# Stores of the inverse's rows moved from SP's queue to ScalarE's, and the last two pairs of out tiles loaded by SP inside the loop

## The chip, the cores and the metric

The kernel runs on one core of one Trainium2 chip. Its time is the device time of one execution in microseconds (us); the time before is the median of three executions, 530.65 us (528.84 to 531.64). The profile shown is that of one more execution.

## What is computed

Two branches work on 2048 rows of 512 channels and are mixed by a gate that each row computes for itself. Branch `a` is a long convolution (a state space model): each channel has a filter of 2048 taps, and the product with the signal is made in the frequency domain. Branch `b` is a two-layer network with a gelu between.

```python
x = A_u                                             # 1 x 2048 x 512
g = sigmoid((x * gate_w).sum(-1, keepdims=True))
# a: taps K[d, l] = Re sum_n C[d,n] * exp(dt*A[d,n]*l) * dt*B[d,n];  y = irfft(rfft(u) * rfft(K)) + u * Dskip
a = _A_ref(x, A_re, A_im, B_re, B_im, C_re, C_im, log_dt, Dskip)
h = gelu(einsum("bsd,df->bsf", B_x, w1) + b1)       # F = 1792
b = einsum("bsf,fd->bsd", h, w2) + b2
return g * a + (1 - g) * b
```

## The kernel before

The kernel has two parts. `front` (0 to about 418 us of the profiled span) makes the network, the filter's taps and the first stage of both transforms; a planner sets its order, and nothing in it changes here. It leaves `(1 - g) * b` in the output tensor for most rows, the half-transformed signal in the DRAM tensor `tu_d`, the half-transformed taps in `tk_d`, and a few products of the network (`late`) still to do.

`conv` is written out by hand, in program order, with no planner. Its tiles are 128 x 512 floats (256 KB). It has sixteen steps `s`, each for two of 32 slices, then a tail. In step `s`:

- SP loads what later steps need: tap slices (`fetch`, L1110), constants `cc` (L1102), signal slices (L1241).
- `product(s)`, on VectorE: six operations on the signal `pu` (PSUM) and the taps `k`.
- `signal(s + 1)`, on TensorE (L1129): eight matmul rows of the trace into two PSUM tiles, named `p2u`.
- `matrices(s // 2 + 1)`, in even steps up to 12: ScalarE makes from a `cc` tile the two halves of a matrix `f1` (L1117, L1118, shown as `f`).
- `taps(s + 2)`: TensorE makes `p2k` for `c` = 0 (with a part of `cc`) and `c` = 1 (with `f1`), and ScalarE copies each to `k` (L1137).
- `inverse(s)`: TensorE makes two PSUM tiles `pa` (L1168).
- `turn(s)`: ScalarE copies each `pa` into one of six buffers `sa` (L1174), and SP stores it in the DRAM tensor `t4_d` (L1176; `t_d<-sa` in the profile). After each eighth slice the rows of that group are read back in another layout into `den` and `t3` (L1188): by GpSimd for the first three groups, by ScalarE for the last.
- In steps 7 to 12 SP loads one pair of output tiles back (`dense`, L1202: 512 KB, from the output tensor into a place in `attic` or `loft` whose signal slices are used up). These are the six pairs of `HERE`.

After the loop ScalarE issues the loads of the two pairs in `THERE` (pair 4 into `loft`, pair 5 into `attic`), and TensorE does 18 of the left-over products of the network (L1213 to L1215; three more are done in step 15). Then for each of eight pairs `m` TensorE makes two tiles `pb` (L1273) out of `den` or `t3`, VectorE (L1285) or ScalarE with GpSimd (L1282, L1283) add them to the pair's tiles, and the pair is stored in the output: by SP (L1289), the last pair half by SP and half by ScalarE (L1287).

PSUM has one buffer for each of `p2k` 0 and 1 and `pa` 0 and 1; `k` and `f1` have two buffers each.

An engine runs its instructions in program order, and a DMA that it issues is one of them. What an instruction has to wait for are semaphores. The program deals the DMAs that SP and ScalarE issue round eight of these, called DMAHW0 to DMAHW7, in the order in which the program was laid out; a DMA waits until the one before it on its semaphore, eight DMAs earlier, has landed, unless its engine has already waited for that one.

Of the kernel before, what the change touches and what calls it, by code (L numbers as in the profile page):

```python
# [73 lines left out]
HERE, THERE = (7, 6, 0, 1, 2, 3), (4, 5)  # L74
# [201 lines left out]
def gated_mix(  # L276
# [18 lines left out]
    nc = tc.nc  # L295
# [5 lines left out]
    t4_d = dr.tile([4, 2, GROUP, 2, 32, D], F32, name="t4_d")  # L301
# [789 lines left out]
    def conv(pool, ps, late, attic, loft, den):  # L1091


        sas = [pool.tile([P, D], F32, name=f"sa{k}", bufs=1) for k in range(6)]
# [75 lines left out]
        def turn(s):  # L1170

            for n in (2 * s, 2 * s + 1):
                sa = sas[n % 6]
                nc.scalar.copy(sa, pas.pop(n))  # L1174
                g, k = divmod(n, GROUP)
                nc.sync.dma_start(t4_d[g, :, k].rearrange("e c q d -> (c q) e d"), sa)  # L1176
                if k < GROUP - 1:
                    continue
                rows = t4_d[g].rearrange("e k c q d -> (e k c) q d")

                for h in (0, 4, 8, 16, 24) if g == 3 else (0, 8, 16, 24):
                    if h == 24 and g < 2:
                        held.append((t3[g:P:4, 16:24], rows[:, 24:32]))
                        continue
                    on = nc.gpsimd if n < 31 else nc.scalar
                    e = h + (4 if g == 3 and h < 8 else 8)
                    to = t3[g:P:4, h - 8 : e - 8] if h > 7 else den[g:P:4, h:e]
                    on.dma_start(to, rows[:, h:e])  # L1188
# [4 lines left out]
        def dense(k, on):  # L1193

            q = HERE.index(k) if k in HERE else 6 + THERE.index(k)
            r = 5 + 2 * q if q < 7 else 0
            if r < N_ATTIC:
                mos[k] = attic[:, r : r + 2]
            else:
                r -= N_ATTIC  # L1200
                mos[k] = loft[:, r * D : (r + 2) * D].rearrange("p (s d) -> p s d", s=2)
            on.dma_start(mos[k], out[2 * k : 2 * k + 2].rearrange("s p d -> p s d"))  # L1202

        def rest(n):

            while late and n:
                s, h, l, w, wl = late.pop(0)
                first = s not in accs
                last = not any(e[0] == s for e in late)
                if first:  # L1210
                    accs[s] = ps.tile([P, D], F32, tag=f"pu{s}" if s > 1 else f"pk{s}", name=f"acc{s}", bufs=1)
                ss = slice(s % 2 * P, s % 2 * P + P)
                nc.tensor.matmul(accs[s], h[:, ss], w, start=first, stop=False)  # L1213
                nc.tensor.matmul(accs[s], h[:, ss], wl, start=False, stop=False)
                nc.tensor.matmul(accs[s], l[:, ss], w, start=False, stop=last)  # L1215
                n -= 1
# [13 lines left out]
        for s in range(16):  # L1230

            for n in range(2 * s + N_TK + (2 if s else 0), 2 * s + N_TK + 4):
                if n < 24:
                    fetch(n if n < 16 else n + 8)
            if s == 0:
                for n in range(16, 24):
                    fetch(n)
            if s in (2, 4, 6, 8):
                consts(s // 2 + 3)
            for n in range(2 * s + N_ROOM, min(2 * s + N_ROOM + 2, 32)) if s > 3 else ():  # L1240
                nc.sync.dma_start(us[n], tu_d[ko[n]])  # L1241
            product(s)
            if s + 1 < 16:
                signal(s + 1)
            if s + 2 < 16:
                if s % 2 == 0:
                    matrices(s // 2 + 1)
                taps(s + 2)
            if s == 9:
                for to, rows in held:  # L1250
                    nc.gpsimd.dma_start(to, rows)
            if s == 15:
                rest(N_REST)
            inverse(s)
            turn(s)
            if 7 <= s < 13:
                dense(HERE[s - 7], nc.sync)
        for k in THERE:
            dense(k, nc.scalar)
        rest(18)  # L1260

        for s in range(4):
            m, i = 7 - s // 2, s % 2
            z, g = mos[m][:, i], gate[:, 1, 2 * m + i : 2 * m + i + 1]
            nc.vector.scalar_tensor_tensor(z, accs[s], g, z, ALU.mult, ALU.add)

        for m in range(8):
# [9 lines left out]
            for i in range(2):  # L1277
                t = 2 * m + i
                z, g = mos[m][:, i], gate[:, 0, t : t + 1]
# [21 lines left out]
    with (  # L1301
        tc.tile_pool(name="fp", bufs=2, reuse_waits="tile") as fp,
        tc.tile_pool(name="ps_f", bufs=2, space=PSUM, reuse_waits="tile") as ps_f,
    ):
        conv(fp, ps_f, late, attic, loft, den)
# [64 lines left out]
```

## Time and profile before

| | us |
|---|---|
| median of three executions | 530.65 (528.84 to 531.64) |
| the profiled execution | 528.3 |
| its span | 526.5 |
| TensorE (PE) busy in the span | 509.1 (97%) |
| VectorE (DVE) busy | 428.4 (81%) |
| ScalarE (ACT) busy | 353.0 (67%) |
| GpSimd (POOL) busy | 41.6 (8%) |
| `conv`: first `p2k` matmul to last `pb` matmul | 418.3 to 520.0 |

The columns of a timeline row are the start and the length in us from the span's start, the engine, the line, the operation and its tiles, how many are merged in the row, and in brackets how long the engine was idle just before and what ended that. PE is the matmul side of TensorE, PEld its weight loads; SPq and ACTq are instructions of the SP and ScalarE queues that only issue DMAs or wait, and they are not counted as busy. Buffer numbers are left out of names, so `t` is `t3` or its like, and `t_d` is `t4_d`. Rows of DMAs give how many, the size of one and the median time from issue to landing.

### The profile page before, as it was taken

The numbers are of one execution on the slowest core, as the hardware profiler recorded it, in microseconds if no ns is written. First come the engines' busy times: TensorE is split into PE (matmuls) and PEld (weight loads), VectorE is DVE, ScalarE is ACT, GpSimd is POOL, SyncE is SP. The second block draws the span as 40 slices with busy tenths as digits, with TensorE's granted clock in tenths as the row PEclk, the third lists the DMA queues.
The fourth block names the chain that finished last, engine by engine and source line by source line (L and its number), as shares of the span: only waits on it lengthen the run. The fifth ranks groups of instructions, "written<-read, shape, count | busy, mean of one in ns | idle before, by whom it ended". The sixth has DMA issues, their size and how long they took to land.

```text
span 526.5 us, 12296 instructions
## 1 busy us (share of the span) xinstructions
PE 509.1 (97%) x4858; PEld 387.8 (74%) x4858; DVE 428.4 (81%) x808; ACT 353.0 (67%) x614; POOL 41.6 (8%) x80
## 2 busy tenths in 40 slices
PE   8887999999999999999999999999999999999995
PEld 7656789898889978976988998988988722222551
DVE  6898899999999968879999989999901188777543
ACT  4989946699875689986595998456534545565311
POOL 2000000000000000000012001202010100110123
PEclk9999999999999999999999999999999999999998
DMA  8999664152685434392879026625669899999978
GB/s 241 369 301 285 222 223 153 67 202 54 159 224 201 142 91 132 111 300 86 220 156 301 3 81 126 159 40 121 201 202 172 226 309 319 366 347 375 301 277 329
DMA packets 82517, 107.87 MB, mean 205 GB/s; under 512 B 39334, under 2 KB 43562, under 8 KB 81916
## 3 DMA queue, kind: packets, MB, share of 16 engines
q1 hardware_dynamic: 76476, 85.04, 50.8%
q0 software_dynamic: 5056, 18.65, 14.0%
q10 hardware_dynamic: 928, 3.41, 1.8%
q8 instruction: 38, 0.62, 0.5%
q14 instruction: 19, 0.16, 0.1%
HBM read 61.46 MB, written 45.62 MB: 203 GB/s over the span
## 4 chain that ended last, share of the span: by engine, by line
PE 75%; ACT 11%; DMA 8%; DVE 3%; issue 2%; SPq 1%; ACTq 0%; DVEq 0%
PE pk L693 10%; PE ph L915 8%; PE ph L917 8%; PE ph L916 8%; PE acc L965 8%; PE acc L967 7%; PE acc L966 7%; PE p2u L1129 6%; PE p2k L1129 5%; PE pa L1168 3%; PE pb L1273 3%; DMA tu_d<-attic 2%; PE ph L415 2%; ACT L932 2%; ACT ph L932 2%
## 5 line engine op out<-in xcount | busy, mean ns | idle before, releaser
L915 PE MATMUL ph<-xh,wh 128*128 128x256 f32 x448 | 128.1, 286 | 2.9 <-ACT attic L433 1.8
L917 PE MATMUL ph<-xh,wl 128*128 128x256 f32 x448 | 127.0, 284 | 0.5 <-DVE wl L794 0.4
L916 PE MATMUL ph<-xlo,wh 128*128 128x256 f32 x448 | 126.6, 283 | 0.0
L915 PEld LDWEIGHTS ph<-xh,wh 128*128 128x128 f32 x448 | 85.1, 190 | 11.9 <-issue 5.6
L916 PEld LDWEIGHTS ph<-xlo,wh 128*128 128x128 f32 x448 | 85.2, 190 | 2.0
L917 PEld LDWEIGHTS ph<-xh,wl 128*128 128x128 f32 x448 | 85.1, 190 | 1.2 <-DVE wl L794 1.2
L965 PE MATMUL acc<-wh,hh 128*128 128x512 f32 x206 | 82.9, 403 | 1.3 <-ACT hh L935 1.2
L967 PE MATMUL acc<-wh,hl 128*128 128x512 f32 x206 | 81.1, 394 | 0.4 <-DVE hl L945 0.4
L966 PE MATMUL acc<-wl,hh 128*128 128x512 f32 x206 | 80.9, 393 | 0.0
L932 ACT ACTIVATE ph<-ph,b1t 128x256 f32<-128x256 f32 x112 | 50.4, 450 | 43.3 <-PE ph L917 41.3
L945 DVE TENSOR_TENSOR hl<-ph,hh 128x512 fp32r<-128x512 f32 (+1 forms) x62 | 38.3, 618 | 31.9 <-ACT hh L935 31.6
L693 PE MATMUL pk<-y,den 128*32 128x64 f32 x2048 | 61.4, 290 | 0.0
L693 PEld LDWEIGHTS pk<-y,den 128*32 128x32 f32 x2048 | 57.2, 136 | 3.7 <-issue 1.4
L965 PEld LDWEIGHTS acc<-wh,hh 128*128 128x128 f32 x206 | 38.7, 188 | 15.9 <-issue 6.8
L967 PEld LDWEIGHTS acc<-wh,hl 128*128 128x128 f32 x206 | 38.7, 188 | 10.6 <-DVE hl L945 2.0
L655 DVE TENSOR_TENSOR y<-y,ea 128x64 f32<-128x64 f32 (+4 forms) x80 | 45.2, 566 | 0.2
L966 PEld LDWEIGHTS acc<-wl,hh 128*128 128x128 f32 x206 | 38.7, 188 | 6.5
L935 ACT CAST hh<-ph 128x512 fp32r<-128x512 f32 (+1 forms) x62 | 33.0, 533 | 8.7 <-PE acc L966 5.2
L500 DVE TENSOR_TENSOR loft<-den,zz 128x256 f32<-128x256 f32 (+2 forms) x48 | 37.2, 775 | 1.7 <-ACT den L626 1.3
L501 DVE TENSOR_TENSOR loft<-den,zz 128x256 f32<-128x256 f32 (+2 forms) x48 | 37.1, 773 | 0.0
L668 DVE TENSOR_TENSOR y<-y,loft 128x2048 f32<-128x2048 f32 x16 | 36.5, 2283 | 0.0
L1137 ACT COPY k<-p2k 128x512 f32<-128x512 f32 x32 | 18.8, 586 | 24.9 <-issue 13.1
(183 smaller groups left out, 885.2 us busy)
## 6 DMA issues: line engine op xcount, KB each, us to landing
tu_d<-attic SPq DMA_DIRECT2D x64, 128.0 KB, 3.6
tk_d<-sk SPq DMA_DIRECT2D x32, 256.0 KB, 4.7
t_d<-sa SPq DMA_DIRECT2D x32, 256.0 KB, 6.8
tk<-tk_d SPq DMA_DIRECT2D x24, 256.0 KB, 4.9
t<-t_d POOLq DMA_DIRECT2D x9, 512.0 KB, 8.3
attic<-in_xt_dram SPq DMA_DIRECT2D x16, 256.0 KB, 4.4
xh_d<-xh SPq DMA_DIRECT2D x8, 512.0 KB, 3.2
xl_d<-xlo SPq DMA_DIRECT2D x8, 512.0 KB, 4.9
```

What stands on the lines that cost most here:

```text
L500: vec(2 * m, lambda: vv.tensor_mul(t, a, br), due, [ka, *kb], [kt])
L655: nc.vector.tensor_mul(both(n, 64 - 3 * n, n), both(0, 64 - n, n), an)
L693: nc.tensor.matmul(pks[q][32 * j : 32 * j + 32, :, gg], x[:, r, :, ch], y[:, r, :, ch], start=(r == 0), stop=(r == 1), skip_group_check=True,)
L915: nc.tensor.matmul(p, h, xh[xk][:, d], start=(d == 0), stop=False)
L916: nc.tensor.matmul(p, h, xlo[xk][:, d], start=False, stop=False)
L917: nc.tensor.matmul(p, lo, xh[xk][:, d], start=False, stop=(d == 3))
L932: nc.scalar.activation(phs[q][:, n], phs[q][:, n], AF.Gelu_apprx_tanh, bias=b1t[:, f : f + 1])
L945: nc.vector.tensor_sub(lo, phs[q][:, 0:nf], hi.bitcast(F32))
L965: nc.tensor.matmul(a, h, wh[1][w], start=start, stop=False)
L966: nc.tensor.matmul(a, h, wl[1][w], start=False, stop=False)
L967: nc.tensor.matmul(a, l, wh[1][w], start=False, stop=(j == 3))
L1129: nc.tensor.matmul(out[64 * i : 64 * i + 64], w, x, start=True, stop=True)
```

## The change

`turn` first makes both copies, and then ScalarE itself issues both stores. SP issues none of them any more. The two loads of `THERE` go from ScalarE, after the loop, to SP, at the ends of steps 14 and 15.

```diff
@@ turn(s)
             for n in (2 * s, 2 * s + 1):
                 sa = sas[n % 6]
                 nc.scalar.copy(sa, pas.pop(n))
+            for n in (2 * s, 2 * s + 1):
                 g, k = divmod(n, GROUP)
-                nc.sync.dma_start(t4_d[g, :, k].rearrange("e c q d -> (c q) e d"), sa)
+                nc.scalar.dma_start(t4_d[g, :, k].rearrange("e c q d -> (c q) e d"), sas[n % 6])
                 if k < GROUP - 1:
                     continue
                 rows = t4_d[g].rearrange("e k c q d -> (e k c) q d")
@@ the loop over s
             turn(s)
             if 7 <= s < 13:
                 dense(HERE[s - 7], nc.sync)
-        for k in THERE:
-            dense(k, nc.scalar)
+            if s > 13:
+                dense(THERE[s - 14], nc.sync)
         rest(18)
```

Three places in the built program show what moves. The first is ScalarE at the end of step 1 and the start of step 2, where the copies to `sa` are followed by the two halves of `f`. Before:

```order
L1174 COPY sa_4794<-pa_4937 128x512 [waits PE_49]
L1174 COPY sa_4795<-pa_4940 128x512 [waits PE_49]
L1117 ACTIVATE f_4967<-cc_4814 64x256 [waits DMAHW0_49]
L1118 COPY f_4967<-cc_4814 64x256
L1137 COPY k_4973<-p2k_4970 128x512 [waits DVE_49,PE_49,Activation_49]
```

After:

```order
L1174 COPY sa_4794<-pa_4937 128x512 [waits PE_49]
L1174 COPY sa_4795<-pa_4940 128x512 [waits PE_49]
L1177 DMA t_d<-sa_4794 64x2x512 [waits DMAHW2_49,Activation_49]
L1177 DMA t_d<-sa_4795 64x2x512 [waits DMAHW3_49,Activation_49]
L1117 ACTIVATE f_4967<-cc_4814 64x256 [waits DMAHW0_49]
L1118 COPY f_4967<-cc_4814 64x256
L1137 COPY k_4973<-p2k_4970 128x512 [waits DVE_49,PE_49]
```

Both stores now stand between the copies and `f`; each waits for its copy and for one of the eight semaphores. In the changed program the DMA that last used DMAHW2 is the seventh of the eight `t3` loads of step 0, which SP issues, and that of DMAHW3 is the second store of step 0. At the end of step 5, the next place of this kind that matters below, the two stores wait for a tap load of SP's in step 5 and for the first store of step 4.

The second place is SP in steps 0 to 2, from the last two `t3` loads on (`tk` are tap slices). Before:

```order
L1110 DMA t_4806<-tk_d 128x512 [waits DMAHW1_49]
L1110 DMA t_4806<-tk_d 128x512 [waits DMAHW2_49]
L1176 DMA t_d<-sa_4792 64x2x512 [waits DMAHW3_49,Activation_49]
L1176 DMA t_d<-sa_4793 64x2x512 [waits DMAHW4_49,Activation_49]
L1110 DMA tk_4909<-tk_d 128x512 [waits DMAHW5_49,PE_49]
L1110 DMA tk_4911<-tk_d 128x512 [waits DMAHW6_49,PE_49]
L1176 DMA t_d<-sa_4794 64x2x512 [waits DMAHW7_49,Activation_49]
L1176 DMA t_d<-sa_4795 64x2x512 [waits DMAHW0_49,Activation_49]
```

After:

```order
L1110 DMA t_4806<-tk_d 128x512 [waits DMAHW2_49]
L1110 DMA t_4806<-tk_d 128x512 [waits DMAHW4_49]
L1110 DMA tk_4909<-tk_d 128x512 [waits DMAHW5_49,PE_49]
L1110 DMA tk_4911<-tk_d 128x512 [waits DMAHW6_49,PE_49]
L1110 DMA tk_4947<-tk_d 128x512 [waits DMAHW7_49,PE_49]
L1110 DMA tk_4949<-tk_d 128x512 [waits DMAHW0_49,PE_49]
```

SP's loads no longer stand behind a wait for ScalarE's copies; they wait only for a semaphore of the eight and for TensorE to be through with the buffer.

The third place is ScalarE behind the last copies of step 15. Before:

```order
L1174 COPY sa_4793<-pa_5469 128x512 [waits DMAHW6_49,PE_49,Activation_49]
L1188 DMA den<-t_d 32x2048 [waits DMAHW3_49,DMAHW4_49,DMAHW2_49,DMAHW5_49,DMAHW1_49,DMAHW0_49]
L1188 DMA den<-t_d 32x2048 [waits DMAHW7_49]
L1188 DMA t_4806<-t_d 32x4096 [waits DMASW6_49,DMASW5_49]
L1188 DMA t_4806<-t_d 32x4096 x2
L1202 DMA loft<-out_dram 128x2x512
L1202 DMA attic<-out_dram 128x2x512
L1282 ACTIVATE sa_4792<-pb_5536,gate 128x512 [waits PE_49,Activation_49]
```

After:

```order
L1174 COPY sa_4793<-pa_5470 128x512 [waits DMAHW0_49,PE_49]
L1177 DMA t_d<-sa_4792 64x2x512 [waits DMAHW6_49,Activation_49]
L1177 DMA t_d<-sa_4793 64x2x512 [waits Activation_49]
L1189 DMA den<-t_d 32x2048 [waits DMAHW5_49,DMAHW6_49,DMAHW4_49,DMAHW7_49,DMAHW3_49,DMAHW2_49]
L1189 DMA den<-t_d 32x2048 [waits DMAHW1_49]
L1189 DMA t_4806<-t_d 32x4096 [waits DMASW6_49,DMASW5_49]
L1189 DMA t_4806<-t_d 32x4096 x2
L1283 ACTIVATE sa_4792<-pb_5536,gate 128x512 [waits PE_49]
```

The two `THERE` loads are gone from behind the reads of the last group; on SP they are now the last two DMAs ahead of the output's stores, with nothing between them and the six `HERE` loads.

## Prediction

> **What bounds the kernel now.** I read the busy times by stretch of the convolution first, then the chain of work that ended last, then the timeline of TensorE and ScalarE over one loop step, then the DMA landings.
>
> ```profile
> 440.00:460.00 20.00, 20.00 (x106) 5.50 (x102) 16.33 (x28) 11.05 (x21) 1.59 (x3) 1.00 0.94 330
> 460.00:480.00 20.00, 20.00 (x108) 5.47 (x108) 16.31 (x27) 11.53 (x23) 2.57 (x5) 1.00 0.98 354
> ...
> 496.51 6.42 DMA t_d<-sa
> ...
> 503.02 2.87 DMA den<-t_d
> ...
> 506.02 13.97 PE pb L1273 x64
> ```
>
> The first two rows are stretches of the loop (length, then busy time of PE, PEld, DVE, ACT, POOL; granted clock; DMA share; GB/s). TensorE is busy for all 20.00 us, so whatever delays it in the loop is lost. ScalarE has 11 of 20 us of work. The DMA engines are 94 to 98% busy. The other rows are the chain: behind the loop it runs over the last copy's store, the read back, then the 64 `pb` matmuls.
>
> **ScalarE's extra work.** The change gives ScalarE two DMA issues per step. At the end of even steps the next thing that ScalarE does is a `k` copy, 1.7 us later. At the end of odd steps `f` comes next, and TensorE needs it soon. One place of each kind, with SP's stores of the first:
>
> ```profile
> 479.83 1.07 ACT L1174 COPY sa<-pa 128x512 f32<-128x512 f32 x2 [0.39 <-PE pa L1168]
> 480.93 0.41 ACT L1117 ACTIVATE f<-cc 64x256 f32<-64x256 f32 x1
> 481.36 0.40 ACT L1118 COPY f<-cc 64x256 f32<-64x256 f32 x1
> 482.62 0.59 ACT L1137 COPY k<-p2k 128x512 f32<-128x512 f32 x1 [0.86 <-ACT f L1118]
> ...
> 481.47 1.03 PE L1129 MATMUL p2k<-tk,cc 128*64 128x512 f32 x4
> 482.33 1.03 PE L1129 MATMUL p2k<-tk,f 128*64 128x512 f32 x4
> 483.29 1.09 PE L1168 MATMUL pa<-v,cc 64*64 64x512 f32 x8
> ...
> 480.45 1.21 SPq L1176 DMA_DIRECT2D t_d<-sa  x2
> 484.44 1.07 ACT L1174 COPY sa<-pa 128x512 f32<-128x512 f32 x2 [0.39 <-PE pa L1168]
> 487.19 0.59 ACT L1137 COPY k<-p2k 128x512 f32<-128x512 f32 x1 [1.68 <-issue]
> ```
>
> `f` is done at 481.76 and TensorE multiplies with it at 482.33: 0.57 us to spare. What a late `f` does, the first `taps` shows, and what an issue costs on ScalarE, the tail shows:
>
> ```profile
> 419.72 0.40 ACT L1118 COPY f<-cc 64x256 f32<-64x256 f32 x1
> 420.17 1.08 PE L1129 MATMUL p2k<-tk,f 128*64 128x512 f32 x4 [0.80 <-ACT f L1118]
> 421.08 1.03 PE L1129 MATMUL p2u<-den,cc 128*64 128x512 f32 x4
> ...
> L1188 ACTq DMA_DIRECT2D t<-t_d x3: 550/615/616, 504.3 to 505.5; - x3
> L1188 ACTq DMA_DIRECT2D den<-t_d x2: 521/559/597, 503.0 to 503.6; - x2
> ...
> L1202 ACTq DMA_DIRECT2D loft<-out_dram x1: 785/785/785, 506.2 to 506.2; - x1
> L1202 ACTq DMA_DIRECT2D attic<-out_dram x1: 652/652/652, 507.0 to 507.0; - x1
> ...
> L1137 ACTq EVENT_SEMAPHORE  x2: 17/1324/2631, 484.5 to 488.0; - x2
> ```
>
> TensorE starts 0.05 us after `f` ends (420.12 to 420.17), and the next block starts 0.91 us later (421.08), where undelayed blocks follow each other by 0.86 (481.47 to 482.33). ScalarE's seven issues of these rows (shortest, median, longest in ns) add up to 4.34 us, 0.62 each; SP's two stores take 1.21 with their gaps, about 0.55 each. ScalarE's own rows are nearer: 1.30 for two, with gaps. The last row says that ScalarE's queue was waiting at 484.5 for the next `k` copy while the two `sa` copies (from 484.44 on) still ran, so its sequencer runs ahead of its engine; the first store can be issued beside the second copy, at 480.45 as on SP. Then both are out at 481.75; `f` starts some 0.06 later and needs 0.83: 482.64. TensorE goes on at 482.69 in place of 482.33, and loses 0.05 more: 0.41. Over six places (ends of steps 1, 3, 5, 7, 9, 11) that is **+2.5 us**. From below: issues of 0.38 (the shortest of ScalarE's, quoted further down) leave `f` in time, 0. From above: if the first issue starts only when both copies are through, at 480.93, each place costs 0.48 more, 5.3 in all. I take the middle value because the waiting row bears on that very question.
>
> At the end of even steps the second issue ends at 484.44 + 0.62 + 1.30 = 486.4 and the `k` copy starts at 487.19: the idle 1.68 us hide it. If that cover went, `k` would come late to `product`, which uses it only in the next step but one.
>
> **The new waits.** Behind a store that waits for its semaphore stand `f`, the `k` copies and the next `sa` copies; TensorE waits for `f` within 0.6 us, for the others within more than 1. So waits count after steps 1 and 5, where what is waited for is young:
>
> ```profile
> 425.67 3.82 SPq L1110 DMA_DIRECT2D t<-tk_d  x8
> 433.80 1.07 ACT L1174 COPY sa<-pa 128x512 f32<-128x512 f32 x2 [0.37 <-PE pa L1168]
> 446.46 1.09 PE L1168 MATMUL pa<-v,cc 64*64 64x512 f32 x8
> 452.21 1.07 ACT L1174 COPY sa<-pa 128x512 f32<-128x512 f32 x2 [0.36 <-PE pa L1168]
> ...
> t<-tk_d SPq DMA_DIRECT2D x2, 256.0 KB, 6.5
> t_d<-sa SPq DMA_DIRECT2D x2, 256.0 KB, 6.8
> ...
> t_d<-sa SPq DMA_DIRECT2D x2, 256.0 KB, 8.7
> tk<-tk_d SPq DMA_DIRECT2D x2, 256.0 KB, 8.7
> ```
>
> The landings are those of 429 to 433 and of 447 to 451. Step 1: the seventh `t` load goes out at 425.67 + 6 x 0.48 = 428.5 and lands by its row at 435.0; ScalarE reaches its store at 433.80 + 0.62 = 434.4: 0.6 us. The second store waits for one issued a step (4.6) before it, at 430.4, which lands by its row at 437.2, and is reached at 435.0: 2.2 if a store lands no sooner than now. Step 5: the tap load can go out at 447.1, when TensorE is through with `taps(6)` (446.46) and SP with the one before: 455.8 by the row, against 452.8 when ScalarE is there, 3.0; the store of step 4 (448.2) gives 456.9 against 453.5, 3.4. So the upper end is 2.2 + 3.4 = 5.6. The lower is 0: in a queue of their own the stores do not stand behind SP's loads, and SP's loads no longer stand behind waits for copies, so that all of them may land well inside 4.6 us, a step. I take the smaller wait of step 1 (0.6) and, in step 5, about half of the row's (1.4): **+2.0 us**. After other steps what is waited for is a step or more older, or was waited for by the copy.
>
> **SP.** Removing 32 stores and their waits costs nothing and lets loads go out up to 2.4 us sooner; TensorE, busy throughout the loop, waits for no load there now, so this buys nothing. `HERE` and `THERE` pairs go out when TensorE has used up their places (up to 10 us sooner than now); nothing reads them before the tail.
>
> **The tail.**
>
> ```profile
> 506.02 3.65 PE L1273 MATMUL pb<-den,g1t 128*64 128x512 f32 x16 [0.42 <-DMA den<-t_d]
> 520.36 0.37 SPq L1289 DMA_DIRECT2D out_dram<-attic  x1
> 520.80 0.38 ACTq L1287 DMA_DIRECT2D out_dram<-attic  x1
> 520.83 0.42 SPq L1287 DMA_DIRECT2D out_dram<-attic  x1
> ...
> 520.00:522.00 2.00, 0.00 (x0) 0.00 (x0) 0.75 (x1) 0.00 (x0) 0.33 (x1) 1.00 0.97 375
> 522.00:524.00 2.00, 0.00 (x0) 0.00 (x0) 0.00 (x0) 0.00 (x0) 0.00 (x0) 0.74 1.03 393
> 524.00:526.00 2.00, 0.00 (x0) 0.00 (x0) 0.00 (x0) 0.00 (x0) 0.00 (x0) 0.50 0.18 67
> ```
>
> TensorE waits 0.42 us for the first read back. With the store landing one us sooner than its 6.42 this goes: -0.4, at most -0.6, at least 0. At the end DMA is full: from 520.36 on 0.375 x 1640 + 0.393 x 2000 + 0.067 x 2000 = 1.53 MB move, of which 1.05 MB are stores issued from then on; 0.48 MB is backlog, 1.2 us at 400 GB/s. The `THERE` loads (1.05 MB at 506) are out of the tail, so most of that backlog should go: I take -0.8, between 0 and -1.2. Together **-1.2 us**.
>
> The Trainium skill, "DMA: Bandwidth & Descriptors", section "Issuing engines are not separate DMA queues", says that all queues end on the same 16 engines and that issuing from several saves only the issue time. By that the stores land no sooner and the 0.4 stays; the trace before has no store in ScalarE's queue to test it.
>
> **Sum.** +2.5 + 2.0 - 1.2 = +3.3 us on the profiled execution's 528.3, which is 2.35 below the median; on the median, 530.65 + 3.3 = **534.0 us**, +0.6%.
>
> **The rivals.**
> - *The cover holds.* Issues of 0.55 (1.21 for two) cost 0.32 per place, and no wait is young: 1.9 - 1.2 = +0.7, 531.4 us; with 0.41 per place, 532.0. For it: `f` has 0.57 us to spare and one of two issues lies beside a copy. Against: ScalarE's longer issues and the landing rows.
> - *Faster: the tail pays in full.* 1.05 MB less at the end, 2.6 us at 400 GB/s, and the gap of 0.6, with `f` in time (ScalarE's pair under 0.9 us, from where `f` is not late): 527.4. Against: the stores of the last three pairs cannot be issued before their `pb`.
> - *No running ahead.* Both issues after both copies: 5.3 + 2.0 - 1.2 = +6.1, 536.8. The waiting row speaks against it.
> - *The two queues take turns at issuing.* After steps 1, 3 and 5 SP issues loads at the same time; if each of ScalarE's issues waited for one of SP's (0.55), three places would cost 1.1 more: +6.6, 537.3. Against: the last two stores at 520.80 and 520.83 go out side by side in 0.38 and 0.42. The Trainium skill, "Perfetto Trace Analysis", section "DMA Instruction — HWDGE (DVE, Sync)", says that the descriptor generator is shared and locked for one DMA at a time; the trace here does not agree.
> - *It does not do what it says:* stores land as late as now. That takes 0.4 from the tail and adds waits; it lies inside the range.
>
> **Chances and range.** Under 0.5% (2.65 us) this kernel's runs, which spread over 2.8 us, tell nothing. The forecast 0.40, no running ahead 0.10, taking turns 0.10: slower 0.60. The cover holds: 0.28, within 0.5%. Faster 0.12. The range leaves out the tail's full pay and the case that both 5.3 and 5.6 come together (+9.7): 529.3 to 538.5; the likeliest case alone has 532.5 to 536.
>
> **What would show it.** Right: in the changed profile TensorE waits 0.2 to 0.6 us for `f` in six steps, issues of `t_d` on ACTq of 0.55 to 0.7 us, and ScalarE waits for DMAs ahead of the stores of steps 1 and 5. The `pb` matmuls follow the last `acc` matmul without a gap, and the last store lands about 0.8 us sooner after them. Wrong: no wait for `f` (faster, or no change), or waits at many stores, since a store's semaphore is shared with loads that I took for old.

## The result, and the profile after

| | before | after |
|---|---|---|
| median, us | 528.84 (525.62 to 531.64, 9 executions) | 534.29 (532.34 to 536.52, 9 executions) |
| ratio | | 1.0101, 95% interval 1.0077 to 1.0125 |
| profiled execution, us | 528.3 | 534.32 |
| its span, us | 526.5 | 532.5 |

The changed kernel is slower by 1.0%, 5.3 us with an interval of 4.1 to 6.6. The forecast was 534.0 us and +3.3. So the time agrees better than the difference does: the median of before that the forecast was added to (530.65, three executions) lies 1.8 us above that of the nine executions here.

The loop is where the time goes. This table is worked out from the rows of the `sa` copies in the timelines: the interval from the first copy of one step to that of the next, less the same interval in the profile of before (4.60 us nearly everywhere). Steps that are not named differ by 0.01 or less, except that step 13 is 0.04 shorter and step 14 too.

| delay behind the stores of step | 1 | 3 | 5 | 6 | 7 | 9 | 11 | all |
|---|---|---|---|---|---|---|---|---|
| after, us | 3.16 | 0.27 | 1.27 | 0.18 | 1.09 | 0.40 | 0.31 | 6.6 |

The stretch 430 to 440 of the changed kernel, a row by stretch of the columns known from the prediction, and then the same place in the timeline (the end of step 1):

```profile
430.00:440.00 10.00, 7.24 (x36) 1.88 (x34) 7.87 (x13) 3.97 (x8) 0.00 (x0) 1.00 0.99 351
```

```profile
430.58 1.27 ACTq L1177 DMA_DIRECT2D t_d<-sa  x2
434.57 1.07 ACT L1174 COPY sa<-pa 128x512 f32<-128x512 f32 x2 [0.42 <-PE pa L1168]
435.30 3.96 ACTq L1177 DMA_DIRECT2D t_d<-sa  x2
439.30 0.41 ACT L1117 ACTIVATE f<-cc 64x256 f32<-64x256 f32 x1 [3.66 <-DMA tk<-tk_d]
439.73 0.40 ACT L1118 COPY f<-cc 64x256 f32<-64x256 f32 x1
440.19 1.08 PE L1129 MATMUL p2k<-tk,f 128*64 128x512 f32 x4 [2.95 <-ACT f L1118]
```

TensorE, busy for every microsecond of the loop before, stands still for 2.95 us. It waits for `f`, `f` waits in ScalarE's queue, and the queue holds two stores that take 3.96 us to get out. The copies were through at 435.64, so it is not these that the stores wait for. The second store went out at the end of that row, at 439.26 less an issue of 0.53, so at 438.7. By the program it waits for the semaphore of the second store of step 0, which was issued at 431.3. The landings of that stretch, a row of the DMA view (430 to 433 us):

```profile
t_d<-sa ACTq DMA_DIRECT2D x2, 256.0 KB, 7.3
```

431.3 + 7.3 = 438.6. The name in the bracket of the `f` row, a tap load, is the profile's inference; that load was issued at 434.47 and by the DMA view took 7.2 us to land (441.6), when `f` had long been made, so `f` did not wait for it.

Steps 5, 6 and 7 of the changed kernel, from the same timeline:

```profile
457.05 2.18 ACTq L1177 DMA_DIRECT2D t_d<-sa  x2
459.27 0.41 ACT L1117 ACTIVATE f<-cc 64x256 f32<-64x256 f32 x1 [1.77 <-DMA t_d<-sa]
460.15 1.08 PE L1129 MATMUL p2k<-t,f 128*64 128x512 f32 x4 [1.06 <-ACT f L1118]
...
462.93 3.12 ACTq L1177 DMA_DIRECT2D t_d<-sa  x2
466.15 1.07 ACT L1137 COPY k<-p2k 128x512 f32<-128x512 f32 x2 [2.76 <-DVE z L1154]
...
468.18 1.53 ACTq L1177 DMA_DIRECT2D t_d<-sa  x2
469.76 0.41 ACT L1117 ACTIVATE f<-cc 64x256 f32<-64x256 f32 x1 [1.56 <-DMA attic<-tu_d]
470.64 1.08 PE L1129 MATMUL p2k<-t,f 128*64 128x512 f32 x4 [1.06 <-ACT f L1118]
```

An undisturbed pair takes 1.21 us; here pairs take 2.18, 3.12 and 1.53. In step 5 the second store waits for the first store of step 4 and in step 7 for a signal load, as the brackets say. In step 6 it waits by the program for a tap load of SP's, and `k` copies stand behind it instead of `f`. ScalarE is idle for 2.76 us ahead of them, but 1.67 us of idle time stand there in an undisturbed step (before the `k` copy of step 4, for one), so they come 1.1 us late, and TensorE loses only 0.18 us.

An undisturbed place (end of step 11), and the groups of waits of the convolution (418 to 500 us; total, times, longest) that answer to it:

```profile
487.01 1.07 ACT L1174 COPY sa<-pa 128x512 f32<-128x512 f32 x2 [0.45 <-PE pa L1168]
487.63 1.21 ACTq L1177 DMA_DIRECT2D t_d<-sa  x2
488.89 0.41 ACT L1117 ACTIVATE f<-cc 64x256 f32<-64x256 f32 x1 [0.80 <-ACT sa L1174]
```

```profile
PEld p2k L1129 <- ACT f L1118: 12.4, 7, 3.8
PE p2k L1129 <- ACT f L1118: 6.1, 5, 2.9
```

The first store goes out at 487.63, beside the second copy, which ends at 488.08. The same groups in the profile of before:

```profile
PEld p2k L1129 <- ACT f L1118: 3.4, 7, 1.7
PE p2k L1129 <- ACT f L1118: 0.8, 1, 0.8
```

The one wait of a matmul there, and the longest of the weight loads, is that of the first `taps`, ahead of step 0; it is in the rows of the changed kernel too. In the steps themselves no matmul waited for `f` before.

The tail of the changed kernel, from its timeline:

```profile
513.01 3.65 PE L1274 MATMUL pb<-den,g1t 128*64 128x512 f32 x16
516.49 10.47 PE L1274 MATMUL pb<-t,g1t 128*64 128x512 f32 x48
...
527.82 0.42 SPq L1288 DMA_DIRECT2D out_dram<-attic  x1
```

The gap ahead of `pb` is gone, and from the last store's issue to the end of the span pass 4.7 us (527.82 to 532.5), where in the profile of before it was 5.7 (520.83 to 526.5).

### The profile page after: what moved, and what is told of

The parts are those of the page before. It is cut to its first block, busy times and chain, and to the rows that moved or that the text cites. A ratio compares the mean times of both kernels' runs of the same rounds, so it can differ in the third digit from the quotient of the medians.

```text
span 532.5 us, 12268 instructions
## 1 busy us (share of the span) xinstructions
PE 513.1 (96%) x4858; PEld 389.2 (73%) x4858; DVE 427.9 (80%) x808; ACT 353.0 (66%) x614; POOL 41.6 (8%) x80
## 4 chain that ended last, share of the span: by engine, by line
PE 74%; ACT 11%; DMA 9%; issue 2%; DVE 2%; SPq 1%; ACTq 0%; DVEq 0%
PE pk L693 10%; PE ph L915 9%; PE ph L916 8%; PE ph L917 8%; PE acc L965 8%; PE acc L967 7%; PE acc L966 7%; DMA attic<-tu_d 3%; PE p2k L1129 3%; PE p2u L1129 3%; PE pb L1274 3%; PE pa L1168 2%; PE ph L415 2%; DMA tu_d<-attic 2%; ACT ph L932 1%
## 5 line engine op out<-in xcount | busy, mean ns | idle before, releaser
L915 PEld LDWEIGHTS ph<-xh,wh 128*128 128x128 f32 x448 | 86.3, 193 | 11.9 <-issue 5.6
L916 PEld LDWEIGHTS ph<-xlo,wh 128*128 128x128 f32 x448 | 86.3, 193 | 2.0
L917 PEld LDWEIGHTS ph<-xh,wl 128*128 128x128 f32 x448 | 86.2, 192 | 1.2 <-DVE wl L794 1.2
```

The lines of the kernel that those rows point to most:

```text
L915: nc.tensor.matmul(p, h, xh[xk][:, d], start=(d == 0), stop=False)
L916: nc.tensor.matmul(p, h, xlo[xk][:, d], start=False, stop=False)
L917: nc.tensor.matmul(p, lo, xh[xk][:, d], start=False, stop=(d == 3))
```

## The experiments

Theory A is: a store at the end of a step stands in ScalarE's queue ahead of `f`; it costs 0.3 to 0.4 us where it only takes its issue, and as much more as it waits for a DMA that has not landed. Rival B is that the loss comes from the DMA engines, since SP's loads and the stores are no longer in one line, or from the issues at an even price. All ratios are to the kernel before, run on the same chip.

### The stores alone

```diff
-            if s > 13:
-                dense(THERE[s - 14], nc.sync)
+        for k in THERE:
+            dense(k, nc.scalar)
```

> Only the stores move to ScalarE; the two THERE loads stay on ScalarE behind the reads of the last group. Theory A (the loss is made on ScalarE's queue: each store pair delays f by 0.3 us after odd steps, and stores wait for young DMAs on their semaphore after steps 1, 5, 6 and 7, 4.9 us in all): the loop loses the same 6.5 us, and the tail gains only the gap before the first pb matmul (0.4), so the kernel is 0.5 to 1.5 us slower than the changed one, +6 us against before (ratio 1.011 to 1.014). Theory B (the THERE loads, now in the loop, crowd the DMA engines and that delays the stores and f): without them the loop loses clearly less, and the ratio falls under 1.006.

533.21 us, ratio 1.0108 (1.0079 to 1.0137). The delays behind steps 1, 3, 5, 7, 9 and 11 are 2.29, 0.28, 0.36, 0.68, 0.28 and 0.33 us, 4.1 with the end of the loop, where 6.5 was expected: in this profile, of the fastest of the four executions, the stores of steps 5 to 7 waited less. By the time the whole loss comes from the stores.

### The two THERE loads alone

The kernel before, with the two loads on SP in steps 14 and 15.

```diff
-        for k in THERE:
-            dense(k, nc.scalar)
+            if s > 13:
+                dense(THERE[s - 14], nc.sync)
```

> Only the two THERE loads move to SP in steps 14 and 15; SP still issues the stores. Theory A: nothing in the loop changes; SP issues the two loads between the last stores, so the last store of step 15 may land later or as now, and the output's stores find 1.05 MB less ahead of them: 0.5 to 1 us faster, ratio 0.998 to 0.999, hard to tell from 1. In the profile the span from the end of the last pb matmul to the end is 0.5 to 1.2 us shorter than the 6.5 of before. Theory B (THERE in the loop costs): slower by 1 us or more.

528.52 us, ratio 1.0016 (0.9998 to 1.0034). The loop is undisturbed. From the last store's issue to the end are 4.7 us as in the changed kernel, and yet the time is not shorter. The gap ahead of `pb` is still there:

```profile
507.61 3.65 PE L1273 MATMUL pb<-den,g1t 128*64 128x512 f32 x16 [0.47 <-DMA den<-t_d]
```

### The stores behind f

The changed kernel, but after the odd steps up to 11 the stores are issued behind `f` of the next step.

```diff
@@ turn(s)
+            if s % 2 and s < 12:
+                return
+            stores(s)
+
+        def stores(s):
             for n in (2 * s, 2 * s + 1):
                 g, k = divmod(n, GROUP)
@@ where matrices is called
                     matrices(s // 2 + 1)
+                    if s:
+                        stores(s - 1)
```

> As the changed kernel, but after odd steps ScalarE makes f first and issues the two stores behind it. Theory A: f is never late, so the six places of 0.3 us are gone, and the waits at the stores of steps 1 and 5 now delay only k copies, which have over 1.5 us to spare: at least 5 of the 6.5 us of the loop come back, ratio 0.996 to 1.003. In the profile TensorE has no wait for f in the loop. Theory C (ScalarE's issues or the waits hold up TensorE by way of k or sa as well): half or more of the loss stays, ratio over 1.005.

529.43 us, ratio 1.0019 (1.0000 to 1.0038). Nearly the whole loss is gone with a change of order alone: same queue, same 32 issues. The end of step 1 in its timeline:

```profile
434.40 1.07 ACT L1174 COPY sa<-pa 128x512 f32<-128x512 f32 x2 [0.42 <-PE pa L1168]
435.02 0.53 ACTq L1183 DMA_DIRECT2D t_d<-sa  x1
435.50 0.41 ACT L1117 ACTIVATE f<-cc 64x256 f32<-64x256 f32 x1
435.93 0.40 ACT L1118 COPY f<-cc 64x256 f32<-64x256 f32 x1
437.72 0.54 ACTq L1183 DMA_DIRECT2D t_d<-sa  x1
```

The second store is again 2.2 us late, for the same reason (the second store of step 0 lands at 437.6), but `f` is through before it. In program order both halves of `f` precede the first store; the row shows that store going out at 435.02, before `f` starts, so the queue hands compute instructions to the engine and goes on to DMAs while they wait there.

### The stores of the last steps alone

```diff
-                nc.scalar.dma_start(t4_d[g, :, k]...
+                (nc.scalar if s > 11 else nc.sync).dma_start(t4_d[g, :, k]...
```

> As the changed kernel, but ScalarE issues the stores only from step 12 on, behind the last f; SP issues those of steps 0 to 11. Theory A: no place is left where f stands behind a store and no store on ScalarE waits for a young DMA, so the loop is as before and the tail's gain stays: 1 to 1.5 us faster than before, ratio 0.997 to 0.998. Theory B or C: no faster than before.

528.98 us, ratio 1.0019 (0.9999 to 1.0039). Here stands everything that was to make the tail shorter, the last stores in a queue of their own and the `THERE` loads out of the way, and nothing of what costs in the loop. `pb` starts without a gap, the last 4.7 us are as in the changed kernel, and the time is not shorter.

### The kernel before, once more

Only the two `THERE` numbers are written out.

> The kernel before, with nothing changed but the way the two THERE numbers are written. Ratio 1.000 within 0.2%. It shows how much the start of the first sa copy (429.20 us in the profile of before, 429.80 to 431.43 in those of the changed kernels) differs from one execution to another of the same program. If it comes at 430 to 431 here, the shorter tails of the earlier experiments are a gain that the front's noise hides; if at 429.2 again, the front itself is slower in the changed programs.

528.91 us, ratio 0.9995 (0.9974 to 1.0017). Its timeline:

```profile
431.19 1.07 ACT L1174 COPY sa<-pa 128x512 f32<-128x512 f32 x2 [0.36 <-DMA t<-tk_d]
...
507.53 3.65 PE L1273 MATMUL pb<-den,g1t 128*64 128x512 f32 x16
511.01 10.47 PE L1273 MATMUL pb<-t,g1t 128*64 128x512 f32 x48
...
522.35 0.42 SPq L1287 DMA_DIRECT2D out_dram<-attic  x1
```

This program has no gap ahead of `pb` either in this execution, and 4.7 us from the last issue to the end of its span of 527.1. Neither of the two things that the tail term of the forecast was to remove is there in every execution of the kernel. The gap of 0.4 to 0.5 us stands in two of the four profiles of this study in which SP issues the last stores, and in none of the eight in which ScalarE does, so that the change may take some 0.2 us off the mean there; the times cannot show so little. The end of 5.7 us stands in the first profile of before alone. And its loop begins at 431.19, where the first profile had 429.20. Over all profiles of the study, whose fronts hold the same code, it begins between 427.48 and 431.43.

### Half of the stores

ScalarE's stores in one half of the steps: steps 0 to 7 (an edit of the kernel before, so that `THERE` stays on ScalarE), and steps 8 to 15 (an edit of the changed kernel).

```diff
+            for n in (2 * s, 2 * s + 1):
                 g, k = divmod(n, GROUP)
-                nc.sync.dma_start(t4_d[g, :, k]..., sa)
+                (nc.scalar if s < 8 else nc.sync).dma_start(t4_d[g, :, k]..., sas[n % 6])
```

> ScalarE issues the stores of steps 0 to 7, SP those of steps 8 to 15, and the THERE loads stay where they were before. Theory A (a store at the end of a step holds ScalarE's queue until the DMA eight places earlier has landed, and the transforms' f behind it comes late): the waits all fall in steps 1, 5, 6 and 7, so nearly the whole loss stays: sa copies of step 8 about 5.5 to 6 us later against the first copy than in the kernel before, then 4.60 us a step; about 533 to 534.5 us. Theory B (the loss is 32 issues on ScalarE at an even price): half the loss, about 531. The tail is that of the kernel before in both.

535.55 us, ratio 1.0110 (1.0077 to 1.0143): the whole loss from half of the stores. An even price per issue is out.

```diff
-                nc.scalar.dma_start(t4_d[g, :, k]...
+                (nc.scalar if s > 7 else nc.sync).dma_start(t4_d[g, :, k]...
```

> SP issues the stores of steps 0 to 7, ScalarE those of steps 8 to 15; the THERE loads are SP's. Theory A: two places where f stands behind the issues are left (ends of steps 9 and 11), 0.3 us each, and no wait for a young DMA: the sa copies of steps 10 and 12 come 0.3 us late, all else in 4.60; +0.6 us, ratio 1.000 to 1.003. Theory B (even price for each of the 32 issues): half the loss, 1.005.

528.33 us, ratio 1.0005 (0.9987 to 1.0023). The delays behind steps 9 and 11 are 0.28 and 0.72 us, where 0.3 each was expected. The second holds a wait for a load of output tiles:

```profile
480.99 1.61 ACTq L1177 DMA_DIRECT2D t_d<-sa  x2
482.65 0.41 ACT L1117 ACTIVATE f<-cc 64x256 f32<-64x256 f32 x1 [1.20 <-DMA loft<-out_dram]
```

The first of the two had in step 1 the largest delay of all, 4.88 us, and 1.17 more in step 2. Its TensorE, by the timeline and by stretches:

```profile
437.60 1.98 PE L1129 MATMUL p2k<-tk,f 128*64 128x512 f32 x4 [2.86 <-ACT f L1118]
439.51 1.99 PE L1168 MATMUL pa<-v,cc 64*64 64x512 f32 x8
441.43 1.98 PE L1129 MATMUL p2u<-attic,cc 128*64 128x512 f32 x4
443.19 1.35 PE L1129 MATMUL p2u<-attic,f 128*64 128x512 f32 x4
444.37 1.02 PE L1129 MATMUL p2k<-tk,cc 128*64 128x512 f32 x4
```

```profile
434.00:438.00 4.00, 1.14 (x6) 0.30 (x4) 2.83 (x5) 1.24 (x3) 0.00 (x0) 0.88 1.00 383
438.00:442.00 4.00, 4.00 (x14) 0.60 (x12) 0.00 (x0) 1.19 (x3) 0.00 (x0) 0.50 0.39 117
442.00:446.00 4.00, 4.00 (x16) 1.03 (x12) 2.48 (x5) 1.16 (x3) 0.00 (x0) 0.77 0.44 167
```

The wait itself was 2.86 us. Behind it TensorE's granted clock is 0.50 for some six microseconds, and its blocks take 1.98 us where they took 1.03 to 1.09: about 3 us more in steps 1 and 2 together (4.88 + 1.17 - 2.86 = 3.2). The other steps have only the price of the issues, 0.28, 0.34 and 0.29 us behind steps 3, 5 and 7. So in this profile, of the fastest of the four executions, the waits that were expected in steps 5 to 7 did not come, and the lower clock makes up for them; the size of the loss was forecast for another reason.

### The t3 loads spread

The changed kernel, with the eight loads that SP issues in step 0 spread over four steps. The second store of step 1 then comes to wait for the first store of step 0.

```diff
-            if s == 0:
-                for n in range(16, 24):
+            if s < 4:
+                for n in range(2 * s + 16, 2 * s + 18):
                     fetch(n)
```

> The changed kernel, with the eight t3 loads of step 0 spread two a step over steps 0 to 3. Step 1's second store then waits for the first store of step 0 (about 4.4 us old when it is reached) in place of the second. Theory A with crowded landings: step 0's stores took 7.3 us to land because eight t3 loads were issued just ahead of them; with six of these gone they land in about 3 to 5 us, and the delay between the sa copies of steps 1 and 2 falls from 3.16 us to between 0.3 and 1; about 531.5 to 532.5 us. If a store takes 7 us however few loads stand ahead of it, the delay stays at about 3 and the time at 534. Steps 5 to 7 keep their delays of 1.27, 0.18 and 1.09 in both.

532.45 us, ratio 1.0065 (1.0042 to 1.0088). The delay of step 1 is 1.45 us, half of what it was, and the trace names the store:

```profile
434.58 2.35 ACTq L1177 DMA_DIRECT2D t_d<-sa  x2
436.98 0.41 ACT L1117 ACTIVATE f<-cc 64x256 f32<-64x256 f32 x1 [1.94 <-DMA t_d<-sa]
```

It waited until about 436.4 for a store issued at 429.98: a landing of 6.4 us, in place of 7.3. The expectation's 3 to 5 us did not come. The delay shrank by 1.7 us: 0.9 for the landing, and some 0.7 because the store waited for is the first of its pair and so that much older. With six of the eight loads gone a landing still takes 6.4 us, so their crowd explains little of the 7.3; each figure is that of one execution. Other steps moved as well: the delay of step 3 rose to 0.82 and that of step 6 to 0.54 us.

### ScalarE from step 2 on

```diff
-                nc.scalar.dma_start(t4_d[g, :, k]...
+                (nc.scalar if s > 1 else nc.sync).dma_start(t4_d[g, :, k]...
```

> SP issues the stores of steps 0 and 1, ScalarE those of all later steps; the THERE loads are SP's. Theory A: step 1's delay of 3.16 us (2.3 to 4.9 in the three kernels that have it) is gone, 4.60 us a step up to step 3, and the later delays stay (some 3.5 us): ratio about 1.006 to 1.007 in place of 1.010. If step 1 only passed its delay on from the DMA engines' load, the next step with a store on ScalarE would take it over, and the ratio stays at 1.010.

532.24 us, ratio 1.0082 (1.0051 to 1.0112). Step 1 has no delay; steps 3, 5, 6, 7, 9 and 11 have 0.28, 1.09, 0.12, 1.57, 0.65 and 0.32 us. No other step takes over the delay of step 1, yet steps 5 to 9 have 0.5 more than in the changed kernel. The interval holds the expected 1.006 to 1.007, and 1.010 as well; the single delays tell the two apart, the ratio does not.

### GpSimd issues the stores

```diff
-                nc.scalar.dma_start(t4_d[g, :, k]...
+                nc.gpsimd.dma_start(t4_d[g, :, k]...
```

> The changed kernel, with all stores issued by GpSimd in place of ScalarE, the THERE loads on SP. Stores and loads share neither a queue nor the eight semaphores, as little as SP's work can wait for a copy. Theory A (what costs is ScalarE's queue in front of f): no wait for f, 4.60 us a step throughout, about 526.5 to 529.5 us. Theory B (what costs is that loads and stores run into each other once SP no longer puts them in one line): the delays of steps 1 and 5 to 7 stay, 532 us or more.

531.67 us, ratio 1.0045 (1.0025 to 1.0066): between the two expectations. Step 1 has no delay and no matmul waits for `f` up to step 6. But ScalarE now waits for the stores:

```profile
461.25 0.59 ACT L1174 COPY sa<-pa 128x512 f32<-128x512 f32 x1 [1.17 <-DMA t_d<-sa]
...
498.85 1.21 ACT L1174 COPY sa<-pa 128x512 f32<-128x512 f32 x2 [6.13 <-DMA t_d<-sa]
...
506.44 3.65 PE L1274 MATMUL pb<-den,g1t 128*64 128x512 f32 x16 [1.18 <-DMA den<-t_d]
```

A copy needs a buffer whose store, three steps older, must be through. At 461.25 that costs 0.6 us of the loop. Ahead of the last step it makes the copies 3.9 us late (498.85, 7.21 after those of step 14 in place of 3.32), so the last store is late and `pb` waits 1.18 us. GpSimd's queue also holds the read backs of finished groups, and behind one of them stand the stores of step 12, whose copies began at 484.11:

```profile
489.46 0.54 POOL L1189 DMA_DIRECT2D den<-t_d  x1 [7.87 <-DMA t_d<-sa]
489.99 1.57 POOL L1189 DMA_DIRECT2D t<-t_d  x3
491.55 3.18 POOL L1177 DMA_DIRECT2D t_d<-sa  x5
```

The read back waits until the stores of its group have landed, and the next group's stores wait with it. So theory A holds for the delays that it named, and it has another form, in another queue; of rival B there is this much in it, that in the loop, where the DMA share from 450 to 490 us is 0.92 or more in stretches of 10 us (one stretch of one kernel has 0.77), landings of 6 to 9 us leave little room to whatever waits for them.

### The changed kernel, once more

One comparison written otherwise.

> The changed kernel once more, with one comparison written otherwise (s >= 14). Ratio 1.010 within 0.25%. The question is how the delays of single steps differ between two executions of one program: those of step 1 (3.16 us in the first profile) and of steps 5 to 7 (1.27, 0.18, 1.09) hang on landings and may move by a us or two, those behind undisturbed issues (0.27, 0.40, 0.31) should be the same to 0.05 us. If TensorE's granted clock falls to one half behind the idle time of step 1, as it did with stores on ScalarE in steps 0 to 7 alone (0.50 from 438 to 442 us), the loss of that execution is some 2 us larger.

534.62 us, ratio 1.0129 (1.0086 to 1.0172). Delays behind steps 1, 3, 5, 6, 7, 9 and 11: 3.32, 0.28, 0.54, 1.84, 0.56, 0.51 and 0.29 us. Those of steps 3 and 11 repeat to 0.02 us. That of step 9 does not repeat to 0.05 us, as was expected (0.40 and 0.51). Those of steps 5 to 7 are dealt out anew (2.94 in all, 2.54 in the first profile), since they hang on landings. The clock stayed at 1.00 behind a wait of 3.1 us.

## Why the prediction was right, and where it was not

It was right in its sign, its range and its main mechanism. All three terms were off in size: the first 0.6 too high, the second 2.7 too low by the profile, and the third took off 1.2 that the times do not show. Together they gave +3.3 where 5.3 was measured, and the base of 530.65 was 1.8 too high. That 534.0 came within 0.3 us of the median of 534.29 is luck: the two errors cancel.

- **`f` behind the issues, +2.5.** The mechanism is as predicted: six places, first issue beside the second copy, `f` late by the second. The size is 0.27 to 0.31 us in place of 0.41 (0.40 in step 9, whose pair takes 1.31), because issues on ScalarE take a median of 0.526 us for these stores and 1.18 to 1.21 for a pair; the step that took 0.62 from the tail's issues, which are of other shapes, was wrong, and SP's 1.21 would have been the right row. Six places at 0.31 are 1.9.
- **The new waits, +2.0.** This is the term that was too small: 6.6 - 1.9 = 4.7 us in the first profile, and about 5.4 in the second (7.2 - 1.8), near the upper end of 5.6. By the measured 5.3 us it is some 3.5 (5.3 - 1.8), and the profile of the stores alone has 2.3 (4.1 - 1.8). Step 1 was put at 0.6, by choosing the smaller of two waits; the other, a store issued one step earlier, decides. Its 2.2 us came from a landing of 6.8; this one took 7.3. The hope that stores in a queue of their own land well inside a step failed there. Step 5 was put at 1.4 and gave 0.96 and 0.2. Steps 6 and 7 were not in the sum at all: "what is waited for is a step or more older" was true of age and wrong as a bound, since loads issued from 455 to 458 us took 10 to 12 us to land. The chain of waits of the changed kernel shows the one of step 7:

```profile
457.35 11.76 DMA attic<-tu_d
```

- **SP, at nothing.** The loads did go out sooner, and TensorE gained nothing by it. That SP's loads run ahead while the DMA engines are full may be what stretches those landings; no run holds SP back with the stores on ScalarE, so that is not shown.
- **The tail, -1.2.** In the trace it came as predicted, gap gone and end 1.0 us shorter. But the kernel before has the same tail in its second profile, and the experiments with the tail's change alone do not gain (1.0016 and 1.0019). The term should have been 0 to -0.2: a 0.42 us gap and a backlog of one execution were taken for properties of the kernel. The skill page that was weighed against it there ("DMA: Bandwidth & Descriptors", section "Issuing engines are not separate DMA queues", of the Trainium skill: another issuing queue saves only the issue time) was nearer to the time, since the times show no gain of the tail. For the loop the trace agrees with it only roughly: stores took a median of 6.8 and 6.1 us to land in SP's queue (two profiles) and 5.7 and 5.0 in ScalarE's, so a little sooner, and in step 0, where it counted, 7.3.
- **Sum.** 1.9 + 4.7 + 0 = 6.6, against 5.3 (4.1 to 6.6) by the ratio. The profiled execution lies at the upper edge of what the times allow; that the waits differ by a us between executions is part of it.
- **Rivals.** "No running ahead" is refuted by the first store at 487.63 beside a copy that ends at 488.08. "Taking turns at issuing" too: at the end of step 3, one of its three places, the pair goes out beside two loads of SP's in the 1.18 us that it takes alone, where 1.1 more was to be expected. "The cover holds" was right about the price of a place and wrong about the waits. The sentence on what would make the prediction wrong, that a store's semaphore is shared with loads taken for old, describes steps 6 and 7. The two queues at the end of step 3:

```profile
447.42 0.90 SPq L1242 DMA_DIRECT2D attic<-tu_d  x2
447.56 1.18 ACTq L1177 DMA_DIRECT2D t_d<-sa  x2
```

## What to carry to other kernels

A DMA that a compute engine issues is an instruction in that engine's queue, with its waits: count for each one what stands behind it and how soon that is needed, and put it behind the urgent work, not ahead (here a change of order alone gave back nearly all of 1%). For what it waits for, look up the DMA whose semaphore it shares and give it the longest landing that the stretch shows, not the median, when the DMA engines are full. A gain read from a short gap or a backlog in one profile should be seen in a second profile of the same program first.

## What was not expected of the hardware

- A wait of TensorE may cost about twice its length: behind 2.86 us without a matmul the granted clock was 0.50 from 437.0 to 443.8 us in one kernel, and 1.00 behind 2.95 and 3.1 us in two profiles of another. The Trainium skill, "TensorE: Matmul & The Clock Gate", section "What's actually happening", says that the clock is halved after an idle window of about 3.4 us which runs freely, whatever the kernel does. The drop to 0.50 agrees, and so does a window: in every profile here in which the granted clock changes more than once, it does so only at times that are whole multiples of 3.41 us apart (in this one at 437.0 and 443.8, two windows apart, and in its front at 30.8, 37.6, 44.5 and 47.9). That the window has to be idle does not agree: the one from 433.6 to 437.0 held 2.3 us of the wait, and TensorE was busy in the rest. Carried on from the clock's other changes, an edge lies in the middle of the other two waits (437.2 to 440.2 with an edge at 438.7, and 435.9 to 439.0 with one at 437.6), so that no window held more than 1.7 us of them. This place in the window would explain why one of three similar waits was hit; how much idle time a window must hold is not shown.
- A store of 256 KB took 2.6 to 11.0 us to land in the changed kernel, with a median of 5.7, and the spread of one place between executions sets delays of 0.2 to 1.8 us (step 6).
